# Early buffers in the room of a later weight, half score rounds and urgent adds: one change to a two-layer memory-attention kernel

## The chip, the cores and the metric

The kernel runs on one core of a Trainium2 chip. The metric is device time in microseconds (us) of one execution. A time is a median of several executions; all those quoted of the kernel before and after were in the fast state, and of the experiments all but one. TensorE, VectorE, ScalarE, GpSimd and SyncE are called PE, DVE, ACT, POOL and SP in the profile; PEld is TensorE's weight load. The granted clock is the share of TensorE's full clock that the profile's clock records show.

## The reference

x has 2048 tokens of 640 values. A layer of attention with a compressed memory (A) and a feed-forward layer with relu (B) each add to x; the pair is applied twice with the same weights.

```python
for s in range(4):                                   # segments of L = 512 tokens, 32 heads of 20
    logits = einsum('bhqd,bhkd->bhqk', qs, ks) * scale + mask
    p      = softmax(logits);  a_dot = einsum('bhqk,bhkd->bhqd', p, vs)
    pq     = phi(qs)                                 # t + 1 for t > 0, else exp(t)
    a_mem  = einsum(pq, M) / (einsum(pq, z) + 1e-06)
    o      = g * a_mem + (1 - g) * a_dot
    M, z   = M + einsum(phi(ks), vs), z + sum(phi(ks))
...
x = x + A(layernorm(x)); x = x + B(layernorm(x))     # B: relu(x @ w1) @ w2, 640 -> 1728 -> 640
x = x + A(layernorm(x)); x = x + B(layernorm(x))     # the same weights again
```

What matters here: each segment needs q, k and v, its scores and exps, a memory read (from segment 1 on) and an output projection, before the feed-forward of that segment can start. At the start of the first layer no feed-forward is ready, so TensorE has little to fill waits with.

## The kernel before

The kernel is written as some thirty streams of operations. A scheduler on the host gives each operation a modelled duration, picks at each step the one that can start first (then the one of better rank, then the stream with the lower number), and so fixes the order of every engine's instructions before the launch. An order made with modelled times is therefore part of the kernel.

```python
SEM_NS = 60.0                                # modelled time of a semaphore
...
key = (round(start), prio, n)                # smallest key goes next
```

Storage is handed out in slots; an operation that needs one waits until the last user releases it. The slots of this story:

```python
STG = [[Slot(stg[:, c, n], "stg") for c in range(FC)] for n in range(2)]   # k (n=0), q (n=1), 5 pieces each
VA = [Slot(v_aug[:, k], "va") for k in range(2)]                           # v of two segments
X = Slot(ps[:, 0:2, :], "SX")                # two PSUM banks of scores for two heads
Y = Slot(ps[:, 2:4, :], "SY")                # and two for the other two
MISC = [Slot(ps[:, 5 + k, :], "misc%d" % k) for k in range(3)]
...
sg = yield Acq([STG[n][c]])                  # proj_part: k or q of any segment
...
va = yield Acq([VA[s % 2]])                  # proj_v
```

k's staging piece is released by phi of k; that of q only when both halves of the memory read of that segment are done (`STG[1][c].release(*READ[a, s])`); v when the last heads have used it. A score round is four matmuls with 20 rows (or eight, where two key blocks share the banks), for four heads at once, followed by two exps, one for each pair of banks:

```python
def scores(m):
    ...
        yield Acq([X])
        yield Acq([Y])
        t0, t1 = yield pe(413.0, mms((0, 1, 2, 3)), pd + X.tks + Y.tks)
        for k, (bkp, tk) in enumerate(((X, t0), (Y, t1))):
            ...
            tx = yield act(1024, lambda e, dst=dst, src=src: e.activation(dst, src, ACT.Exp, scale=SCALE), [tk] + pw)
            bkp.release(tx)
```

The weights w1 and w2 of the feed-forward are loaded during the first layer, one piece after each score round's exps. A residual add (`add_half`) takes 320 columns of a PSUM bank into x on VectorE and frees the bank; an evacuation (`evac`) may go to ScalarE or VectorE, whichever is modelled to end first.

The softmax here doesn't subtract the row's maximum and nothing guards it: scores larger than these inputs give would overflow.

Of the kernel before, what the change touches and what calls it, by code (L numbers as in the profile page):

```python
# [11 lines left out]
H = 32  # L12
DH = 20
NSEG = 4
# [95 lines left out]
class Op:  # L110
# [4 lines left out]
    def __init__(self, alts, waits, dma=None, acq=None):  # L115
        self.alts = alts
        self.acq = acq
        self.waits = [t for t in waits if t is not None]
        self.dma = dma

# [18 lines left out]

class Need:  # L140
# [3 lines left out]

SEM_NS = 60.0
# [5 lines left out]
class Sched:  # L151
# [30 lines left out]
    def _settle(self, st):  # L182

        while True:
            self._fill(st)
            if st[4]:
                return False
            y = st[2]
            if isinstance(y, Op):
                return True  # L190
            if isinstance(y, Need):
                if y.key not in self.events:
                    return False
                st[2], st[3] = None, (self.events[y.key],)
            else:
                s = self._pick(y.slots)
                if s is None:
                    return False
                s.free = False
                st[2], st[3] = None, (s,)  # L200
# [20 lines left out]
    def run(self):  # L221
        while True:
            best = None
            moved = True
            while moved:
                moved = False
                for st in self.streams:
                    had = st[2]
                    self._settle(st)
                    if st[2] is not had and not isinstance(st[2], Op):  # L230
                        moved = moved or st[2] is None
            heads = [(st[0], n, st, self._alts(st[2])) for n, st in enumerate(self.streams)
                     if not st[4] and isinstance(st[2], Op)]
            for prio, n, st, alts in heads:
                ok = []
                for end, start, k, e in alts:
                    if not any(p2 < min(prio, HOLDERS) and any(e2 == e and s2 + HOLD_TOL[e] < end for _, s2, _, e2 in al2[:1])
                               for p2, _, _, al2 in heads):
                        ok.append((end, start, k))
                if not ok:  # L240
                    continue
                end, start, k = min(ok)
                key = (round(start), prio, n)
                if best is None or key < best[0]:
                    best = (key, st, end, start, k)
# [6 lines left out]
            _, st, end, start, k = best  # L252
            op = st[2]
            e, hold, fns, tail = op.alts[k]
            waits, slot = op.waits, None
            if op.acq is not None:
                slot = self._pick(op.acq)
                slot.free = False
                waits = waits + slot.tks
                fns = [(lambda eng, fn=fn, slot=slot: fn(eng, slot), mark) for fn, mark in fns]  # L260
# [20 lines left out]
def pe(ns, fns, waits=(), acq=None):  # L281
    return Op([("pe", ns, fns, 190.0)], waits, acq=acq)
# [6 lines left out]
def dve(n, mode, fn, waits=(), extra=0.0, acq=None):  # L289
    return Op([("dve", 66.0 + n / (0.96 * mode) + extra, [(fn, True)], 95.0)], waits, acq=acq)  # L290
# [6 lines left out]
def evac(n, mode, vfn, afn, waits=(), psum=True):  # L297
    return Op([("act", (52.0 if psum else 94.0) + n / 1.2, [(afn, True)], 125.0),
               ("dve", 66.0 + n / (0.96 * mode), [(vfn, True)], 95.0)], waits)
# [12 lines left out]
def bass_interleave_layers__memory_aug_infini_attn__dense_activation_relu__prompt_kernel(  # L312
    nc, A_x, A_wq, A_wk, A_wv, A_wo, A_beta, B_x, B_w1, B_w2, out,
):
    with contextlib.ExitStack() as es:
# [53 lines left out]
        STG = [[Slot(stg[:, c, n], "stg") for c in range(FC)] for n in range(2)]  # L369
# [8 lines left out]
        VA = [Slot(v_aug[:, k], "va") for k in range(2)]  # L378
# [42 lines left out]
        def late_loads():  # L421
# [16 lines left out]
            pieces += [half(k, h) for k in range(FC) for h in range(2)]  # L438
            pieces += [rows("w2", w2_r, B_w2, k) for k in range(NFULL)]
# [7 lines left out]
            for n, (name, nbytes, fn) in enumerate(pieces):  # L447
                if name not in sems:
                    sems[name] = sem_("d_" + name)
                w = yield Need("ex", *divmod(n, 5))  # L450
                tk = yield dma("sp", sems[name], nbytes, fn, w[:1] + z1, issue=400.0, lat=4500.0)
                left[name] -= 1
                if left[name] == 0:
                    S.set(name, tks=[tk])

        def consts():
# [29 lines left out]
            for b in range(2):  # L486
                VA[b].tks = [t2]
# [195 lines left out]
        def proj_part(a, s, c, n, h):  # L683
# [9 lines left out]
            if (a, s, c, n) not in QK:  # L693
                sg = yield Acq([STG[n][c]])
                QK[a, s, c, n] = (sg, [])
# [32 lines left out]

        def proj_v(a, s):
            xt = yield Need("xts", a, s)  # L730
            xt = xt[0]
            va = yield Acq([VA[s % 2]])
# [21 lines left out]
        def spill(a, s):  # L754
            for c in range(FC):
# [7 lines left out]
                for n in range(2):  # L763
# [4 lines left out]
                    scr[s % 2, 128 * c:128 * c + 128, :], stg[:, c].rearrange("p n t -> p (n t)")),  # L768
# [54 lines left out]
        def phi_(n):  # L823
            def f(a, s):
                if s == (NSEG - 1, 0)[n]:
                    for c in range(FC):
                        p = yield Need("packed", a, s, c)
                        STG[n][c].release(*p)
                    return
                done = []  # L830
                for c in range(FC):
# [3 lines left out]
                    q = stg[:, c, n, :]  # L835
# [9 lines left out]
                    if n == 0:  # L845
                        STG[0][c].release(tp)
                        if c in (2, 4):
                            S.set("phk", a, s, c // 3, tks=done)
                            done = []
# [4 lines left out]
        READ = {}  # L854

        def mem_read(hb):
            def f(a, s):
# [8 lines left out]
                for i in range(NJ):  # L866
                    fns = []
                    for z, (c, h0, h1) in enumerate(lst):
                        fns.append((lambda e, bk, c=c, h0=h0, h1=h1, z=z, i=i: e.matmul(  # L869
                            bk.ap[:, (h0 - 16 * hb) * 21:(h1 - 16 * hb) * 21],  # L870
                            stg[:, c, 1, i * 128:(i + 1) * 128],
# [16 lines left out]
                if len(READ[a, s]) == 2:  # L888
                    for c in range(FC):
                        STG[1][c].release(*READ[a, s])  # L890
                    BDS.release(*READ[a, s])
# [12 lines left out]
        def mem_write(a, s):  # L904
            mg = yield Need("maskg")
            if s < NSEG - 1:
# [3 lines left out]
                for p, cs in enumerate(PARTS):  # L910
# [4 lines left out]
                    for i in range(NJ):  # L915
                        fns = []
                        for c in cs:
                            fns.append((lambda e, b=None, c=c, i=i, o0=o0, st=(i == 0 and c == cs[0]), bk=bk: e.matmul(  # L918
                                (b or bk).ap[:, CH_OFF[c] - o0:CH_OFF[c + 1] - o0], phk[:, c, i, :],
                                v_aug[:, s % 2, i, CH_H0[c]:CH_H1[c], :].rearrange("p h e -> p (h e)"),  # L920
# [30 lines left out]
        def scores(m):  # L951
            a, r = divmod(2 * m, NSEG * G)
            s, g = divmod(r, G)
            pts = []
            sl = pd = None
            for u, parts in enumerate(ROUNDS):
                if u in (0, 2):
                    pt = yield Acq([PTS[u // 2]])
                    pts.append(pt)
                if u == 0:  # L960
                    pd = yield Need("pad", a, s, g)
                    sl, pd = pd[0], pd[1:]
                elif u == 2:
                    p1 = yield Need("pad", a, s, g + 1)
                    pd = pd + p1[1:]
                pw = [t for z, _, _ in parts for t in pts[z].tks]

                def mms(heads):
                    fns = []
                    for y, (z, j, o) in enumerate(parts):  # L970
                        N = L - 128 * j
                        for hh in heads:
                            fns.append((lambda e, z=z, j=j, hh=hh, N=N, o=o: e.matmul(  # L973
                                ps[:, hh, o:o + N], sl.ap[32 * hh:32 * hh + DH, z, 0, 128 * j:128 * j + 128],
                                sl.ap[32 * hh:32 * hh + DH, z, 1, 128 * j:L]),
                                y == len(parts) - 1 and hh in (1, 3)))
                    return fns

                yield Acq([X])
                yield Acq([Y])  # L980
                t0, t1 = yield pe(413.0, mms((0, 1, 2, 3)), pd + X.tks + Y.tks)
                ex = []
                for k, (bkp, tk) in enumerate(((X, t0), (Y, t1))):
                    if u == 2:
                        dst = PT[:, :, 2 * k:2 * k + 2, PT_OFF[2]:PT_OFF[2] + 256].rearrange("p z h q -> p h z q")
                        src = bkp.ap.rearrange("p h (z q) -> p h z q", z=2)
                    else:
                        c0 = PT_OFF[parts[0][1]]
                        dst = pts[parts[0][0]].ap[:, 2 * k:2 * k + 2, c0:c0 + 512]
                        src = bkp.ap  # L990
                    tx = yield act(1024, lambda e, dst=dst, src=src: e.activation(dst, src, ACT.Exp, scale=SCALE),  # L991
                                   [tk] + pw)
                    bkp.release(tx)
                    ex.append(tx)
                S.set("ex", m, u, tks=ex)
            sl.release(t0, t1)
# [15 lines left out]
        def apply(n):  # L1012
# [10 lines left out]
            for i in range(NJ):  # L1023
                for h2 in range(2):
                    fns = []
                    for hh in (2 * h2, 2 * h2 + 1):
                        for j in range(i + 1):
                            fns.append((lambda e, i=i, hh=hh, j=j: e.matmul(  # L1028
                                od[:, i, hh, :], pt.ap[:, hh, PT_OFF[j] + 128 * (i - j):PT_OFF[j] + 128 * (i - j) + 128],
                                v_aug[:, s % 2, j, 4 * g + hh, :], start=(j == 0), stop=(j == i)),  # L1030
# [13 lines left out]
            if g == G - 1:  # L1044
                dmt = yield Need("dm", a, s)
                VA[s % 2].release(tk, *dmt)

# [19 lines left out]
        def add_half(t, hf, bk, tk, waits=()):  # L1067
            ta = yield dve(320, 1, lambda e: e.tensor_tensor(  # L1068
                x_sb[:, t, 320 * hf:320 * hf + 320], x_sb[:, t, 320 * hf:320 * hf + 320], bk.ap[:, 0:320], ALU.add),
                [tk] + list(waits))  # L1070
# [81 lines left out]
        S.add(0, items(scores, NSEG * G))  # L1152
# [60 lines left out]
```

## Time and profile before

| | before |
|---|---|
| time, median of the first three runs | 608.51 us (608.08 to 611.05) |
| span of the profiled run | 607.5 us |
| TensorE busy | 585.3 us, 96% |
| TensorE idle, 40 to 90 us | 7.4 us |
| first feed-forward's first matmul | 111.2 us |
| mean granted clock | 0.989 |

Read it from the engine that is nearly always busy: TensorE. The amount of matmul work is fixed (6474 matmuls), so only its idle time and its low clock can be won back, and the largest piece of that lies between 40 and 90 us. The prediction below shows the lines. Two more of the kernel before are needed later. Both are of TensorE's timeline (start, duration, engine, line of the source, operation, output and input, size, count, and in brackets the idle time before it and who ended it), late in the run:

```profile
386.65 0.30 PE L525 MATMUL ps<-wo_r,oT 128*128 128x320 bf16 x1 [0.92 <-DVE x_sb L1068]
...
410.59 0.40 PE L973 MATMUL ps<-pad 20*128 20x256 bf16 x8 [1.24 <-ACT PT L991]
```

Here TensorE waits 0.92 us for a residual add to free its bank and 1.24 us for exps to free a score bank.

### The profile page before, as it was taken

To read this page: it belongs to the slowest core of one execution; us is meant where nothing else is said; L and a number is where in the kernel's file an instruction comes from. 1 tells how busy PE (TensorE), PEld (TensorE's weight loads), DVE (VectorE), ACT (ScalarE), POOL (GpSimd) and SP (SyncE) were. 2 spreads that over 40 slices of the span, in tenths; PEclk is the share of its full clock that TensorE was granted. 3 is DMA by queue.
4 is the path that set the end of the run, shared out by engine and by line. 5 is a ranking of instruction groups with operands and counts; after the bars stand their busy time and mean duration, and the time that the engine had idled before them with its cause. 6 is when DMAs were issued, how large, how long until landed. Compare 5 with 4: busy or idle time off the path is not lost.

```text
span 607.5 us, 15242 instructions
## 1 busy us (share of the span) xinstructions
PE 585.3 (96%) x6474; PEld 341.6 (56%) x6474; DVE 387.1 (64%) x1053; ACT 410.8 (68%) x520; POOL 185.7 (31%) x292
## 2 busy tenths in 40 slices
PE   7998789999999999999999999999999899999998
PEld 6664355445656554665555655456555564665655
DVE  5867789866877776876358963699636855450202
ACT  5698968978687778767868777586765867304040
POOL 4233433333434333435313442034421443100000
PEclk8999969999999999999999999999999999999999
DMA  8558974943240505611058120740214400401201
GB/s 250 133 134 225 213 162 92 215 99 63 45 151 25 89 1 159 118 31 35 11 138 149 21 44 1 201 105 1 44 36 146 90 27 12 98 34 20 67 1 44
DMA packets 100309, 53.65 MB, mean 88 GB/s; under 512 B 79186, under 2 KB 90130, under 8 KB 100242
## 3 DMA queue, kind: packets, MB, share of 16 engines
q1 hardware_dynamic: 100112, 52.52, 36.8%
q8 instruction: 51, 0.84, 0.6%
q10 hardware_dynamic: 130, 0.16, 0.1%
q14 instruction: 16, 0.13, 0.1%
HBM read 20.49 MB, written 12.85 MB: 55 GB/s over the span
## 4 chain that ended last, share of the span: by engine, by line
PE 76%; DVE 12%; ACT 5%; DMA 4%; POOL 1%; ACTq 1%; issue 1%
PE ps L528 48%; PE ps L525 10%; PE ps L1028 8%; PE ps L973 7%; ACT PT L991 3%; DVE stats L536 3%; DVE xn_tok L578 2%; DMA scr<-stg 2%; PE ps L869 1%; PE ps L918 1%; DVE x_sb L1068 1%; ACT stg L840 1%; DMA phk<-phs 1%; DVE o_sb L1039 1%; DVE om_sb L880 1%; POOL rstd L550 1%
## 5 line engine op out<-in xcount | busy, mean ns | idle before, releaser
L991 ACT ACTIVATE PT<-ps 128x1024 bf16<-128x1024 f32 x320 | 310.3, 1023 | 90.3 <-PE ps L973 85.7
L1004 POOL TENSOR_SCALAR_AFFINE_SELECT PT<-PT 128x512 bf16<-128x512 bf16 x256 | 163.5, 656 | 312.5 <-ACT PT L991 312.5
L528 PE MATMUL ps<-w_r,hT 128*128 128x320 bf16 x832 | 132.0, 299 | 0.0
L528 PE MATMUL ps<-xnT,w_r 128*128 128x512 bf16 x448 | 125.3, 379 | 0.0
L1068 DVE TENSOR_TENSOR x_sb<-x_sb,ps 128x320 bf16<-128x320 bf16 x128 | 60.8, 479 | 84.6 <-PE ps L528 84.0
L528 PEld LDWEIGHTS ps<-w_r,hT 128*128 128x128 bf16 x832 | 78.2, 98 | 33.5 <-issue 5.0
L1028 PEld LDWEIGHTS ps<-v_aug,PT 128*128 128x128 bf16 x2560 | 73.1, 96 | 9.4 <-POOL PT L1004 2.9
L1028 PE MATMUL ps<-v_aug,PT 128*128 128x21 bf16 x2560 | 74.5, 172 | 0.3 <-POOL PT L1004 0.3
L1119 ACT ACTIVATE hT<-ps 128x512 bf16<-128x512 f32 x57 | 34.1, 598 | 55.1 <-PE ps L528 54.8
L973 PE MATMUL ps<-pad 20*128 20x512 bf16 (+3 forms) x1024 | 64.0, 303 | 7.2 <-ACT PT L991 7.1
L528 PEld LDWEIGHTS ps<-xnT,w_r 128*128 128x128 bf16 x448 | 42.3, 98 | 46.8 <-issue 5.9
L536 DVE BATCH_NORM_STATS2 stats<-x_sb 128x6 f32<-128x320 bf16 x124 | 54.5, 473 | 4.6 <-DMA x_sb<-in_A_x_dram 4.2
L973 PEld LDWEIGHTS ps<-pad 20*128 20x128 bf16 x1024 | 17.8, 92 | 58.9 <-ACT PT L991 28.5
L1117 DVE TENSOR_SCALAR hT<-ps 128x512 bf16<-128x512 f32 x55 | 37.5, 684 | 18.4 <-PE ps L528 17.9
L528 PE MATMUL ps<-wo_r,oT 128*128 128x320 bf16 x256 | 47.0, 299 | 0.0
L1036 DVE RECIPROCAL rden<-ps 128x16 f32<-128x16 f32 x64 | 16.2, 253 | 43.3 <-PE ps L1028 43.1
L525 PE MATMUL ps<-xnT,w_r 128*128 128x512 bf16 x112 | 42.6, 380 | 0.2 <-DVE hT L1117 0.2
L840 ACT ACTIVATE stg<-stg 128x512 bf16<-128x512 bf16 x60 | 36.3, 638 | 9.0 <-DVE rtmp L838 8.9
L701 DVE CAST stg<-ps 128x512 bf16<-128x512 f32 (+1 forms) x46 | 28.7, 627 | 17.6 <-PE ps L528 17.4
L528 PE MATMUL ps<-wv_r,xnT 128*128 128x320 bf16 x192 | 36.2, 299 | 0.0
L528 PE MATMUL ps<-xnT,wk_r 128*128 128x512 bf16 (+1 forms) x140 | 35.0, 353 | 0.0
L528 PE MATMUL ps<-xnT,wq_r 128*128 128x512 bf16 (+1 forms) x140 | 34.6, 353 | 0.0
(85 smaller groups left out, 610.1 us busy)
## 6 DMA issues: line engine op xcount, KB each, us to landing
scr<-stg SPq DMA_DIRECT2D x39, 256.0 KB, 3.1
pad<-scr SPq DMA_DIRECT2D x124, 80.0 KB
out_dram<-x_sb SPq DMA_DIRECT2D x16, 160.0 KB, 1.8
w_r<-in_B_w_dram SPq DMA_DIRECT2D x10, 216.0 KB, 3.2
w_r<-in_B_w_dram SPq DMA_DIRECT2D x13, 160.0 KB, 3.3
x_sb<-in_A_x_dram SPq DMA_DIRECT2D x4, 320.0 KB, 5.5
x_sb<-in_A_x_dram SPq DMA_DIRECT2D x8, 160.0 KB, 3.0
wv_r<-in_A_wv_dram SPq DMA_DIRECT2D x1, 800.0 KB, 8.2
```

The costliest lines, as they stand in the source:

```text
L525: bk, tk = yield pe(mm_ns(n), [(lambda e, bk, a=a, b=b: e.matmul(bk.ap[:, 0:n] if len(b.shape) == 2 else bk.ap[:, 0:n].rearrange("p (i n) ...
L528: tk = yield pe(mm_ns(n), [(lambda e, k=k, a=a, b=b, bk=bk: e.matmul(bk.ap[:, 0:n] if len(b.shape) == 2 else bk.ap[:, 0:n].rearrange("p (i ...
L536: tk = yield dve(320, 1, lambda e, c2=c2: e.bn_stats(stats6[:, t, c2, :], x_sb[:, t, c2 * 320:(c2 + 1) * 320]), xt)
L701: te = yield evac(N, 1, lambda e, sg=sg, bk=bk: e.tensor_copy(sg.ap[:, t0:t0 + N], bk.ap[:, 0:N]), lambda e, sg=sg, bk=bk: e.activation(sg ...
L840: te = yield act(512, lambda e, q=q: e.activation(q, q, ACT.Exp), [tr] + p, psum=False)
L973: fns.append((lambda e, z=z, j=j, hh=hh, N=N, o=o: e.matmul(ps[:, hh, o:o + N], sl.ap[32 * hh:32 * hh + DH, z, 0, 128 * j:128 * j + 128], ...
L991: tx = yield act(1024, lambda e, dst=dst, src=src: e.activation(dst, src, ACT.Exp, scale=SCALE), [tk] + pw)
L1004: tm = yield pool(600.0, lambda e, reg=reg: e.affine_select(out=reg, in_=reg, pattern=[[0, 4], [1, 128]], compare_op=ALU.is_ge, fill=0.0, ...
L1028: fns.append((lambda e, i=i, hh=hh, j=j: e.matmul(od[:, i, hh, :], pt.ap[:, hh, PT_OFF[j] + 128 * (i - j):PT_OFF[j] + 128 * (i - j) + 128] ...
L1068: ta = yield dve(320, 1, lambda e: e.tensor_tensor(x_sb[:, t, 320 * hf:320 * hf + 320], x_sb[:, t, 320 * hf:320 * hf + 320], bk.ap[:, 0:32 ...
L1117: th = yield evac(512, 1, lambda e, dc=dc, bk=bk: e.tensor_scalar(hT[:, dc, :], bk.ap[:, :], 0.0, None, ALU.max), lambda e, dc=dc, bk=bk: ...
L1119: lambda e, dc=dc, bk=bk: e.activation(hT[:, dc, :], bk.ap[:, :], ACT.Relu), [tk] + HT.tks)
```

## The change

The intent is to fill TensorE's early hole. w2 is not needed until the first feed-forward has done its first half, so its space is lent: v of segment 0, and k and q of segment 1, go there. v and q of segment 2 then need not wait for the room. w2 is loaded when those have been used. Besides, a score round may go in halves: as long as the first feed-forward is not ready and TensorE would idle, and at any time when the banks of the other half are taken. And residual adds and evacuations go ahead of other work of the same modelled start. Parts of the diff, cuts marked:

```diff
+LONE_NS = 300.0
...
-                key = (round(start), prio, n)
+                key = (round(start + late), 0.5 if op.urgent else prio, n)
...
+        early_w = w2_r[:].rearrange("p c d -> p (c d)")
+        STGS = [stg, early_w[:, VLEN:VLEN + 2 * FC * L].rearrange("p (c n t) -> p c n t", c=FC, n=2)]
...
+        VAUG = [v_aug[:, k] for k in range(2)]
+        VAUG += [early_w[:, 0:VLEN].rearrange("p (j h e) -> p j h e", j=NJ, e=DH + 1)]
...
+                if n == n2:                            # the first piece of w2
+                    v0 = yield Need("v00")
+                    q1 = yield Need("q01")
+                    w2w = v0 + q1 + early_done
...
+        def vx(a, s):
+            return 2 if (a, s) == (0, 0) else s % 2
+        def sx(a, s):
+            return 1 if (a, s) == (0, 1) else 0
...
-                sg = yield Acq([STG[n][c]])
+                sg = yield Acq([STG[sx(a, s)][n][c]])
...
+                    lone = pe(413.0, [f for fs in a[2] for f in fs], a[1] + a[0].tks, take=[a[0]])
...
+                    both = pe(413.0, fns, a[1] + b[1] + a[0].tks + b[0].tks, take=[a[0], b[0]])
+                    return both, (lone if ("hx", 0, 0) not in S.events and max(ready[0], S.free["pe"]) + LONE_NS < max(ready[1], S.free["pe"]) else None)
...
-                [tk] + list(waits))                    # add_half; evac alike
+                [tk] + list(waits), urgent=True)
```

One detail of the new score stream is easy to miss: it takes "the next half and the one after it" as a pair. After an odd number of lone halves, each pair is the second half of one round and the first half of the next.

## The prediction

> **What bounds the kernel now.** I read the page first, then the busy time by stretch, then the timeline of TensorE inside the bad stretch, and the chain of waits there.
>
> ```profile
> span 607.5 us, 15242 instructions
> PE 585.3 (96%) x6474; PEld 341.6 (56%) x6474; DVE 387.1 (64%) x1053; ACT 410.8 (68%) x520; POOL 185.7 (31%) x292
> ...
> PE   7998789999999999999999999999999899999998
> ```
>
> TensorE is the bound: 96% busy, no other engine above 68%, and slices under 9 only near the start and one late. Since the amount of matmul work does not change, the kernel can only get shorter by what TensorE idles, stalls or runs at a low clock. The stretches say where that is (columns: stretch, its length, busy us of PE, PEld, DVE, ACT, POOL with counts, granted clock, DMA share, GB/s):
>
> ```profile
> 0.00:40.00 40.00, 36.46 (x383) 27.14 (x384) 26.46 (x78) 25.77 (x43) 14.49 (x31) 0.96 0.66 176
> 40.00:90.00 50.00, 42.58 (x549) 22.97 (x547) 39.40 (x114) 42.90 (x56) 20.05 (x30) 0.90 0.80 193
> 90.00:320.00 230.00, 225.63 (x2737) 126.97 (x2736) 163.88 (x435) 179.33 (x217) 83.78 (x129) 1.00 0.38 86
> 320.00:530.00 210.00, 205.88 (x2345) 119.00 (x2344) 138.97 (x384) 146.09 (x178) 66.42 (x101) 1.00 0.31 68
> 530.00:607.50 77.50, 74.75 (x468) 45.54 (x466) 18.43 (x45) 16.72 (x28) 1.01 (x1) 1.00 0.14 38
> ...
> 70.00:80.00 10.00, 6.98 (x130) 4.43 (x122) 8.37 (x29) 8.50 (x10) 4.59 (x8) 0.76 0.75 208
> 80.00:90.00 10.00, 9.81 (x109) 5.77 (x106) 7.21 (x23) 6.15 (x7) 4.00 (x6) 0.73 0.74 148
> ```
>
> Idle TensorE: 3.5 us before 40, 7.4 in 40 to 90, 4.4 in 90 to 320, 4.1 in 320 to 530, 2.8 after. In 70 to 90 the clock was also granted at 0.76 and 0.73, so (0.24 + 0.27) x 10 = 5.1 us of clock are missing. The early hole is thus worth 7.4 + 5.1 = 12.5 us, 2.1% of 608.5, if all of it comes back. The timeline shows what TensorE has to do there:
>
> ```profile
> 58.40 0.39 PE L973 MATMUL ps<-pad 20*128 20x512 bf16 x4 [1.27 <-ACT PT L991]
> ...
> 69.83 0.40 PE L973 MATMUL ps<-pad 20*128 20x256 bf16 x8 [1.09 <-ACT PT L991]
> ...
> 76.33 0.50 PE L869 MATMUL ps<-BD,stg 128*128 128x147 bf16 x3 [1.25 <-DVE om_sb L880]
> ...
> 81.33 0.45 PE L525 MATMUL ps<-wv_r,hT 128*128 128x320 bf16 x1
> ...
> 100.39 0.39 PE L525 MATMUL ps<-hT,wq_r 128*128 128x512 bf16 x1
> ...
> 110.07 0.39 PE L525 MATMUL ps<-xnT,wk_r 128*128 128x512 bf16 x1
> ```
>
> L973 is a score round, L869 the memory read. While TensorE waits for the exps at 58 to 77, the value projection of segment 2 (wv_r,hT) runs only from 81.3, its query projection from 100.4, the key projection of segment 3 from 110.1. Their inputs were there (x of segment 2 was normalized by 49); they had no room to write to. v of segment 2 needs the place of v of segment 0; q of segment 2 needs the staging of q of segment 1, which is held until the memory read is done (its last matmuls of segment 1 are at 96.6). So TensorE starves at 50 to 80 while 8 x 0.68 + 5 x 1.08 = 10.8 us of ready projections wait for buffers. The chain of waits in that stretch is ScalarE's:
>
> ```profile
> 59.38 1.83 ACT PT L991 x2
> 61.21 1.03 ACT stg L840 x2
> 62.24 1.83 ACT PT L991 x2
> ```
>
> Two exps of a round take 1.83 us, then two exps of phi 1.03. The 20 rounds of segment 0 run from 22.0 to 77.1, 2.75 us each; ScalarE is busy 50.4 of these 55 us.
>
> **The skill.** The Trainium skill, "Perfetto Trace Analysis", section Identifying the Most-Contended Engine: busy share of matmuls does not say how near TensorE is to its limit; section Optimization Strategy: repeated bubbles can mean that there is no SBUF or PSUM for the next tile. The trace agrees with both: 0.86 us for four 512-column matmuls in warm streams against 1.07 for four 320-column ones at 81.8, all called busy, and the bubbles are those of staging. "TensorE: Matmul & The Clock Gate", Part 1: idle TensorE falls back to half clock. The trace agrees: full clock until about 70, 0.76 and 0.73 right after idle gaps of 1.1 to 1.3 us in a row. The same page, Part 3: small matmuls on different row groups run at once. It agrees: a round of four 20-row matmuls holds TensorE from 58.40 to 58.73, 0.33 us for all four, and each is 388 ns long. So half a round should take as long as a whole one. The same page's table at the top: VectorE's queue is strict FIFO; no line of the trace shows VectorE's starts overtaking, so an add issued behind statistics waits for them.
>
> **The change part by part.** No matmul, exp or evacuation is added or taken away; one small GpSimd memset is new (under 1 us, GpSimd 31% busy).
>
> 1. Room. v of segment 0 and k, q of segment 1 go to w2's space. Segment 1's staging no longer waits for segment 0's, v and q of segment 2 can run from about 52. That moves 10.8 us of matmuls into 50 to 80, more than the idle there (about 7). But moving work from 81 to 110 into 50 to 80 gains nothing alone, if it leaves a hole at 81 to 110. The right question is what is left when the first feed-forward can start (110.9 now, its first matmul), because from then on there is plenty to fill with. Before: undone at 110.9 and doable earlier is only k of segment 3: 5 x 1.08 = 5.4 us (q of 3 waits for the memory read of 2, v of 3 for segment 1's heads). Its phi, spill and staging come in time for about 3.5 of 5 groups: 3.8 us.
> 2. The first feed-forward comes earlier. The output projection of segment 0 takes 86.8 to 98.1 for 8 x 0.68 = 5.4 us of matmuls, mixed with v of segment 2 (5.4 us); slack 5.8 us, I take half, 3. The exps lose 55 - 50.4 = 4.6 us of ScalarE time; of that I give halves 2. Together 5 us earlier. In these 5 us 1.8 fewer score rounds are done, about 0.8 us of TensorE each with their apply (0.33 + 0.10 switching + 1.0/2.5): -1.5.
> 3. Halves. A lone half costs TensorE another 0.33 us, but only where it idles over 0.3 us by the scheduler's plan: no cost in the hole. Once the first feed-forward is ready they are offered only when the other half's room is taken; I count 0.
> 4. Adds and evacuations first on VectorE. An add takes 0.48 us and holds one of three PSUM banks; the waits that this can shorten are the 0.5 to 1 us ones at 151, 200, 380 before wo and mem matmuls: I take 1.5 of the 8.5 us of idle in 90 to 530.
> 5. w2 last. Its 14 loads go out from 90.0 to 127.9 and its first matmul is at 158. They will now wait for the last memory read of segment 1 (96.6): about 7 us later, with the feed-forward 9 earlier the margin shrinks from 27 to some 11 us. No cost.
>
> Sum: 3.8 + 5 - 1.5 + 0 + 1.5 + 0 = 8.8 us. 608.5 - 8.8 = 599.7; I say 599.5.
>
> **The rivals.** (a) ScalarE and VectorE become the bound of the early part: in 40 to 80 they are busy 36.8 and 32.2 of 40 us, and the work moved in brings 5 x 0.60 + 8 x 0.47 = 6.8 us of evacuations, with phi of segment 2 (0.52 + 0.28 + 0.41 a piece, ten pieces, 12 us) wanting to come too. 11 us are free in both. Then exps or evacuations slip, the feed-forward comes no earlier and only part of k of segment 3 is gained: 603 to 606. For it: ScalarE at 10.0 of 10 in 60 to 70. Against: exps go first, and 30 to 40 has room too. (b) All of the hole comes back, with the clock: 12.5 us and the 1.5 of the adds, 594.5. For it: 10.8 us of ready filler against 7.4 of idle. Against: filler used there is missing at 81 to 110, where TensorE is full now only thanks to it; the idle may just move there. (c) The new order upsets the later stages (a static order made from modelled times): small waits of a us here and there, and half rounds where TensorE does have work: 606 to 610. For it: the late waits at 410 and 480 are of that kind. (d) w2 late: a wait of some us before the first second matmul of the feed-forward. Against: the 11 us of margin.
>
> **Range and chances.** 599.5 is the sum. Low end 594 is (b), high end 605 is (a). 2% is 596.3, to be had only with nearly the whole hole: 0.24. Slower by 2% would take a new stall of over 12 us, for which nothing speaks: 0.01. Within 2%: 0.75.
>
> **What would show it.** TensorE's idle in 40 to 90 under 4 us and the clock there back near 1.0 (part 1); wv_r,hT and hT,wq_r matmuls between 50 and 80; the first xnT,w_r matmul near 106, not 111 (part 2), with k of segment 3 before it; more score groups, of two matmuls each, before that time and few after (part 3); idle of 90 to 530 about 7 instead of 8.5 (part 4); no DMA wait on w2 (part 5). Wrong if a hole as large opens at 80 to 110, if the first feed-forward is not earlier, or if the stretches after 320 are longer than now.

## The result, and the profile after

| | before | after |
|---|---|---|
| median time | 609.67 us (4 runs, 608.08 to 611.05) | 603.33 us (4 runs, 601.17 to 604.4) |
| ratio of fast runs | | 0.9892, 95% interval 0.9851 to 0.9934 |
| span of the profiled run | 607.5 us | 601.9 us |
| first feed-forward's first matmul | 111.2 us | 112.5 us |
| second feed-forward's first matmul | 193.0 us | 185.6 us |

Ratios and their 95% intervals, here and below, are those of the record, from fast runs alone; they are not quite the ratios of the medians. 0.9892 is about 6.6 us: (1 - 0.9892) x 609.67. The profiled runs differ by 5.6 us.

The head of the page after:

```profile
span 601.9 us, 15245 instructions
...
PE 582.9 (97%) x6474; PEld 345.0 (57%) x6474; DVE 381.0 (63%) x1045; ACT 415.9 (69%) x528; POOL 183.9 (31%) x293
...
PE   6999979999999999999999999999999999999998
...
PEclk8999989999999999999999999999999999999999
```

The number of matmuls is as before. After the first slice only one is under 9 near the start (the 7), where there were three in a row (8, 7, 8), and the late 8 has gone. The busy time by stretch after (stretch, its length, busy us of PE, PEld, DVE, ACT, POOL with counts, granted clock, DMA share, GB/s):

```profile
0.00:40.00 40.00, 34.98 (x346) 25.61 (x346) 26.77 (x78) 25.07 (x43) 14.14 (x31) 0.96 0.67 182
40.00:90.00 50.00, 46.61 (x603) 25.24 (x604) 44.45 (x121) 44.50 (x56) 20.84 (x31) 0.96 0.83 196
90.00:320.00 230.00, 224.06 (x2755) 128.57 (x2752) 160.97 (x441) 185.00 (x223) 85.18 (x133) 0.99 0.38 89
320.00:530.00 210.00, 208.04 (x2359) 124.12 (x2357) 131.42 (x366) 144.60 (x180) 62.70 (x98) 1.00 0.30 64
...
70.00:80.00 10.00, 10.00 (x109) 4.86 (x106) 9.96 (x29) 7.73 (x10) 3.31 (x6) 1.00 0.67 186
80.00:90.00 10.00, 6.88 (x111) 3.74 (x111) 8.61 (x27) 9.29 (x12) 5.45 (x8) 0.82 1.06 226
90.00:100.00 10.00, 9.20 (x116) 5.56 (x113) 9.18 (x30) 9.01 (x13) 2.60 (x4) 0.84 0.92 214
```

TensorE idles 3.4 us in 40 to 90 instead of 7.4, and 70 to 80, the emptiest ten before (6.98 busy, clock 0.76), is full at full clock. But the next ten took its place: 6.88 busy in 80 to 90, with a clock of 0.82 there and 0.84 in the ten that follow. TensorE's timeline says what was moved and what then was missing:

```profile
53.79 0.30 PE L559 MATMUL ps<-wv_r,hT 128*128 128x320 bf16 x1
...
65.57 0.38 PE L559 MATMUL ps<-hT,wq_r 128*128 128x512 bf16 x1
...
84.39 0.39 PE L1020 MATMUL ps<-pad 20*128 20x256 bf16 x4 [1.11 <-ACT PT L1072]
...
86.59 0.50 PE L913 MATMUL ps<-BD,w_r 128*128 128x147 bf16 x3 [0.89 <-DVE om_sb L924]
87.02 0.61 PE L1020 MATMUL ps<-pad 20*128 20x512 bf16 x2
...
91.18 0.45 PE L559 MATMUL ps<-wo_r,oT 128*128 128x320 bf16 x1
...
99.43 0.31 PE L559 MATMUL ps<-wo_r,oT 128*128 128x320 bf16 x1 [0.64 <-DVE x_sb L1150]
...
100.12 0.38 PE L559 MATMUL ps<-xnT,wk_r 128*128 128x512 bf16 x1
...
112.52 0.38 PE L559 MATMUL ps<-xnT,w_r 128*128 128x512 bf16 x1 [0.70 <-issue]
...
136.62 0.30 PE L559 MATMUL ps<-w_r,hT 128*128 128x320 bf16 x1
```

The projections v and q of segment 2 (wv_r,hT and hT,wq_r) moved from 81 and 100 to 54 and 66, as intended. The key projection of segment 3 (xnT,wk_r) comes at 100.1, not 110.1, and its five groups are done before the first feed-forward (xnT,w_r); in the kernel before they ran from 110.1 to 126.7, between the feed-forward's. In 84 to 99 TensorE waits for exps, for the memory read's VectorE work and for a residual add. The groups of 4 and 2 small matmuls are lone halves. The first feed-forward is not earlier: 112.52.

w2's loads, in SyncE's list (the program's output name w_r stands for several weights):

```profile
112.00 3.68 SPq L456 DMA_DIRECT2D w_r<-in_B_w_dram  x8
...
126.39 0.56 SPq L468 DMA_DIRECT2D w_r<-in_B_w_dram  x1
```

They are issued from 112.0 to 126.4, and the first matmul that reads w2 is the last line of the timeline above, 136.6; it waited for nothing.

Why the first feed-forward is not earlier is seen where ScalarE works off the exps of segment 0. First the stretch of its 20 score rounds, before (to 77.1) and after (to 79.8):

```profile
22.00:77.10 55.10, 48.48 (x621) 27.18 (x619) 42.10 (x114) 50.46 (x67) 20.72 (x31) 0.98 0.78 189
```

```profile
22.20:79.80 57.60, 57.28 (x678) 33.24 (x678) 48.68 (x128) 49.24 (x64) 20.30 (x31) 1.00 0.77 187
```

Then the longest of what ScalarE waited for, up to and in this stretch (engine, its line, who released it: total us, times, longest), before and after:

```profile
ACT PT L991 <- PE ps L528: 3.9, 1, 3.9
ACT PT L991 <- PE ps L973: 2.2, 3, 0.8
```

```profile
ACT PT L1072 <- PE ps L1020: 7.4, 10, 2.0
```

TensorE is now full there, 57.28 of 57.6 us. ScalarE's idle time in the rounds rose from 55.10 - 50.46 = 4.6 us to 57.60 - 49.24 = 8.4, and most of the rise is exps that wait for score matmuls. The longest wait of each list, 3.9 and 2.0, lies before the first exp; within the rounds these waits rose from 2.2 us to about 5.5. The score matmuls stand in the kernel's order behind the filler. The exps of segment 0 end 2.7 us later than before. What bounded this stage was ScalarE before; in the changed kernel it is TensorE that holds it up.

That filler alone does this is not shown. The experiments below have two kernels that are as full in these rounds (TensorE idle 1.1 us in run 4, 0.9 in run 10) and in which ScalarE idles only 5.2 and 4.2 us; in run 7, which has no filler, it idles 9.3. So how full TensorE is does not decide it alone; where the score matmuls stand in the order may be the rest, which was not tested.

The rest of the way to the first feed-forward adds up so: the first output projection matmul comes 11.4 us after the last exps instead of 9.7, the projection takes 10.8 us instead of 11.3, and from its end to the feed-forward are 10.5 instead of 13.1. In the first of these stretches TensorE waits for VectorE and ScalarE, and ScalarE is busy 10.69 of the 11.4 us, where it was busy 5.08 of 9.7.

Further on, part of the early lead is given back. TensorE's stretches before and after:

```profile
210.00:350.00 140.00, 139.85 (x1704) 80.86 (x1702) 97.76 (x262) 107.60 (x130) 50.42 (x78) 1.00 0.34 72
350.00:530.00 180.00, 176.03 (x1947) 100.08 (x1945) 112.42 (x301) 122.03 (x150) 54.31 (x83) 1.00 0.29 66
```

```profile
210.00:350.00 140.00, 137.31 (x1727) 80.93 (x1724) 97.26 (x265) 109.56 (x130) 51.93 (x81) 1.00 0.32 72
350.00:530.00 180.00, 178.04 (x1928) 103.84 (x1926) 104.64 (x284) 123.30 (x158) 50.91 (x79) 1.00 0.32 68
```

Idle in 210 to 350 rose from 0.15 to 2.69 us; idle in 350 to 530 fell from 3.97 to 1.96. The new gaps stand before matmuls that need a transposed block (a DMA here):

```profile
242.92 0.98 PE L964 MATMUL ps<-v_aug,phk 128*128 128x147 bf16 x12 [1.28 <-DMA phk<-phs]
...
285.11 0.39 PE L559 MATMUL ps<-xnT,wk_r 128*128 128x512 bf16 x1 [0.72 <-DMA xnT<-xn_tok]
```

A count of the matmul work done up to each moment in the two traces puts the changed kernel 4.9 us ahead at 122 us, 6.5 at 206, 2.7 at 324 and 5.6 at the end.

### The profile page after: what moved, and what is told of

It is laid out like the page before. It is cut to its first block, busy times and chain, and to the rows that moved or that the text cites. A ratio compares the mean times of both kernels' runs of the same rounds, so it can differ in the third digit from the quotient of the medians.

```text
span 601.9 us, 15245 instructions
## 1 busy us (share of the span) xinstructions
PE 582.9 (97%) x6474; PEld 345.0 (57%) x6474; DVE 381.0 (63%) x1045; ACT 415.9 (69%) x528; POOL 183.9 (31%) x293
## 4 chain that ended last, share of the span: by engine, by line
PE 80%; DVE 10%; DMA 6%; ACT 2%; issue 1%; POOL 0%; SPq 0%
PE ps L562 50%; PE ps L559 10%; PE ps L1108 9%; PE ps L1020 7%; DMA xnT<-xn_tok 2%; DVE x_sb L1150 2%; DVE stats L570 2%; ACT PT L1072 2%; PE ps L913 1%; DVE xn_tok L612 1%; PE ps L964 1%; DMA scr<-stg 1%; DMA phk<-phs 1%; DMA oT<-o_sb 1%; DVE o_sb L1119 1%
## 5 line engine op out<-in xcount | busy, mean ns | idle before, releaser
L1084 POOL TENSOR_SCALAR_AFFINE_SELECT PT<-PT 128x512 bf16<-128x512 bf16 x256 | 160.8, 646 | 319.4 <-ACT PT L1072 319.4
L562 PE MATMUL ps<-w_r,hT 128*128 128x320 bf16 x832 | 134.5, 299 | 0.0
L562 PE MATMUL ps<-xnT,w_r 128*128 128x512 bf16 x448 | 119.9, 379 | 0.0
L1201 ACT ACTIVATE hT<-ps 128x512 bf16<-128x512 f32 x68 | 40.5, 598 | 54.5 <-PE ps L562 53.7
L1108 PEld LDWEIGHTS ps<-v_aug,PT 128*128 128x128 bf16 x2240 | 63.8, 96 | 14.5 <-issue 9.7
L1108 PE MATMUL ps<-v_aug,PT 128*128 128x21 bf16 x2240 | 68.9, 173 | 0.4 <-POOL PT L1084 0.4
L1020 PE MATMUL ps<-pad 20*128 20x512 bf16 (+3 forms) x1024 | 65.5, 303 | 2.3 <-ACT PT L1072 2.0
L1199 DVE TENSOR_SCALAR hT<-ps 128x512 bf16<-128x512 f32 x44 | 30.2, 689 | 26.3 <-PE ps L562 25.9
L559 PE MATMUL ps<-xnT,w_r 128*128 128x512 bf16 x112 | 42.6, 380 | 0.7 <-issue 0.7
L735 DVE CAST stg<-ps 128x512 bf16<-128x512 f32 (+1 forms) x43 | 26.8, 623 | 12.0 <-PE ps L562 11.5
L881 ACT ACTIVATE stg<-stg 128x512 bf16<-128x512 bf16 x50 | 30.8, 633 | 4.9 <-DVE rtmp L879 4.9
```

The source lines that it names most:

```text
L559: bk, tk = yield pe(mm_ns(n), [(lambda e, bk, a=a, b=b: e.matmul(bk.ap[:, 0:n] if len(b.shape) == 2 else bk.ap[:, 0:n].rearrange("p (i n) ...
L562: tk = yield pe(mm_ns(n), [(lambda e, k=k, a=a, b=b, bk=bk: e.matmul(bk.ap[:, 0:n] if len(b.shape) == 2 else bk.ap[:, 0:n].rearrange("p (i ...
L735: te = yield evac(N, 1, lambda e, sg=sg, bk=bk: e.tensor_copy(sg.ap[:, t0:t0 + N], bk.ap[:, 0:N]), lambda e, sg=sg, bk=bk: e.activation(sg ...
L881: te = yield act(512, lambda e, q=q: e.activation(q, q, ACT.Exp), [tr] + p, psum=False)
L1020: fns.append([(lambda e, z=z, j=j, hh=hh, N=N, o=o, sl=sl: e.matmul(ps[:, hh, o:o + N], sl.ap[32 * hh:32 * hh + DH, z, 0, 128 * j:128 * j ...
L1084: tm = yield pool(600.0, lambda e, reg=reg: e.affine_select(out=reg, in_=reg, pattern=[[0, 4], [1, 128]], compare_op=ALU.is_ge, fill=0.0, ...
```

## The experiments

Theory A was the prediction's: the room is what counts; the time is won at the start, by k of segment 3 getting out of the way of the first feed-forward. Its rivals were that the two helpers (halves, and urgent adds and evacuations) do the work, and theory L: each edit makes another static order, whose small waits fall otherwise by chance, and that is what the time shows. Twelve kernels were run; all gave the reference's result. In the edits, lines of the changed kernel carry a minus. "The room" means both places lent, that of v and that of the staging of k and q.

**Run 1: the room alone, rounds whole, nothing urgent.**

```diff
-                    lone = pe(413.0, [f for fs in a[2] for f in fs], a[1] + a[0].tks, take=[a[0]])
+                    lone = None
-                    return both, (lone if ("hx", 0, 0) not in S.events and ... else None)
+                    return both, None
-                [tk] + list(waits), urgent=True)        # and in evac
+                [tk] + list(waits))
```

> The changed kernel with its buffers in the space of w2 and w2 last, but score rounds whole again and no add or evacuation put first on VectorE. Theory A (the gain is the room: it lets k of segment 3 run before the first feed-forward, 5 x 1.08 = 5.4 us): 0.989 to 0.993 of the kernel before, that is 4 to 6.5 us faster, k of segment 3 (xnT,wk_r matmuls) done before the first xnT,w_r matmul. Theory B (the gain is the score halves and the order on VectorE; the room only moves the hole from 50-80 to 80-90): 0.997 to 1.000.

Measured: 1.0022 of before (1.0003 to 1.0041), median 610.82 against 609.13. The room alone gains nothing; theory A in its simple form has fallen. And yet its early part is there: k of segment 3 is begun at 95.6, and the second feed-forward starts at 186.1 instead of 193.0. The count of matmul work has this kernel 5.3 us ahead at 207 and 0.3 behind at 376. So the gain is made and then given back. Where is in the stretch 210 to 350, whose idle rose to 2.88 us from 0.15, and in the three longest waits of TensorE in it:

```profile
210.00:350.00 140.00, 137.12 (x1729) 78.68 (x1727) 102.68 (x270) 109.32 (x128) 52.91 (x83) 1.00 0.34 72
```

```profile
PE ps L559 <- DMA xnT<-xn_tok: 0.9, 1, 0.9
PE ps L913 <- DVE om_sb L924: 0.9, 2, 0.5
PE ps L964 <- DMA phk<-phs: 0.6, 1, 0.6
```

These are the start of the second layer: normalized x, transposed k and the memory read come to TensorE just too late for an order that runs earlier. At 368.7 there is another of the kind:

```profile
368.74 0.39 PE L559 MATMUL ps<-xnT,wk_r 128*128 128x512 bf16 x1 [1.03 <-DMA xnT<-xn_tok]
```

The added idle of 210 to 350 is 2.7 of the 5.6 us that were lost between 207 and 376, the gap at 368.7 another 1.0; where the rest went was not found.

**Run 2: both helpers, no room.**

```diff
-                if n == n2: ...
-                    w2w = v0 + q1 + early_done
+                w2w = []
...
-            return 2 if (a, s) == (0, 0) else s % 2
+            return s % 2
...
-            return 1 if (a, s) == (0, 1) else 0
+            return 0
```

> The changed kernel with the buffers and the load order of before, but halves and the order on VectorE kept. Theory A (room): 0.997 to 1.001 of the kernel before, the hole at 50 to 80 as before. Theory B (halves and order): 0.989 to 0.993.

Measured: 0.9963 (0.9945 to 0.9981), 606.88. The helpers alone gain 2.3 us. The second feed-forward starts at 195.6, so the gain is not the early one; idle in 350 to 530 fell from 3.97 to 1.70 us, the waits shown at 386 and 410 among it.

**Run 3: the change without halves.** The first two edits of run 1.

> The changed kernel with whole score rounds only. In the changed kernel only three groups of two score matmuls stand alone, but from the first one on the pairs run across rounds (six matmuls). Theory A: halves are worth nothing, the time is that of the changed kernel within 1 us (0.989 +- 0.002 of before). Rival C (the crossed pairs hurt: ScalarE lost 8.3 us in the rounds of segment 0 against 4.6 before): 2 us faster than the changed kernel, 0.985 to 0.987. Rival D (halves help as intended): 2 to 3 us slower, 0.993 to 0.995.

Measured: 0.9923 (0.9894 to 0.9952), 604.52. That is 1.9 us above the whole change (0.9923 - 0.9892 of 609), but the intervals overlap.

**Run 4: the change with nothing urgent.** The last edit of run 1.

> The changed kernel with adds and evacuations in their old rank on VectorE, halves and room kept. The prediction gave the adds 1.5 us: by it 1.5 us slower than the changed kernel, 0.991 to 0.993 of before. Rival: the new rank holds up the statistics and the first feed-forward (at 112.5 in the changed kernel, 110.9 before): 1 to 2 us faster, 0.985 to 0.988, with the first xnT,w_r matmul before 110.

Measured: 0.9892 (0.9868 to 0.9916), 603.12: the same as the whole change. On top of halves the urgent order is worth nothing that shows. But together the two are worth a lot on top of the room: 1.0022 with neither, 0.9892 with both or with halves alone, 0.9923 with urgent alone. The parts do not add up. Room alone is +0.2%, helpers alone -0.4%, both -1.1%. Any one helper keeps most of the early gain.

**Run 5: the change with phi of segment 2 held until the first feed-forward is ready.**

```diff
             def f(a, s):
+                if (a, s) == (0, 2):
+                    yield Need("hx", 0, 0)
```

> The changed kernel, with phi of segment 2 held back until the first feed-forward is ready. Its staging then stays taken, so k of segment 3 can't run before the first feed-forward; the hole at 50 to 80 stays filled as in the changed kernel. Theory A (what is gained early is k of segment 3, 5.4 us): the early lead falls from 5 us to about 0, time 0.996 to 1.000 of before. Rival F (filling the hole at 50 to 80 is itself the gain): stays at 0.988 to 0.991. Rival a of the prediction (phi and evacuations on VectorE and ScalarE hold up the first feed-forward): its first xnT,w_r matmul comes at 109 or earlier instead of 112.5.

This asks two things: whether phi's work on ScalarE and VectorE delays the first feed-forward, and what k of segment 3 ahead of it is worth, because k of segment 3 needs the staging that phi of segment 2 frees. Measured: 0.9954 (0.9938 to 0.997), 606.76. TensorE's timeline:

```profile
109.11 0.61 PE L559 MATMUL ps<-xnT,wk_r 128*128 128x512 bf16 x1
...
111.21 0.63 PE L559 MATMUL ps<-xnT,w_r 128*128 128x512 bf16 x1
```

The first feed-forward comes at 111.2 instead of 112.5. k of segment 3 is not out of the way (it starts at 109.1 and runs on to 124), the second feed-forward starts at 192.4, about as in the kernel before, and 3.8 us of the gain are gone: (0.9954 - 0.9892) x 609.84.

But the edit changed a second thing, and that leaves both questions open. The matmuls above last 0.61 and 0.63 us, those of the same shape in the changed kernel 0.38. The stretch of 90 to 130 in the changed kernel and in this run (the granted clock is the third number from the end):

```profile
90.00:130.00 40.00, 38.09 (x470) 20.65 (x466) 32.23 (x96) 35.10 (x45) 14.72 (x23) 0.96 0.63 149
```

```profile
90.00:130.00 40.00, 36.63 (x420) 18.86 (x418) 31.62 (x94) 33.32 (x42) 15.08 (x24) 0.85 0.63 146
```

The clock records have half clock from 101.9 to 112.1 us here. The mean clock of this run's 22 executions is 0.982 (none above 0.986), that of the changed kernel's four 0.990 (none below 0.989), that of the kernel before in the rounds of run 5 0.991. So the low clock belongs to this order and is no chance, and 0.8% of the time is 4.8 us, if TensorE is busy throughout: as much as was lost. How much of the 3.8 us is k of segment 3 in the way and how much the clock, this run can't tell; nor does the first feed-forward's 1.3 us bound what phi delays, since it too came after the half clock.

**Run 6: the staging's room alone; v stays in its two places.** Both helpers stay.

```diff
-            return 2 if (a, s) == (0, 0) else s % 2
+            return s % 2
...
-                    w2w = v0 + q1 + early_done
+                    w2w = q1 + early_done
```

> The changed kernel with room only for k, q of segment 1; v of segment 0 and 2 share their place as before. Theory A: q of segment 2 and so k of segment 3 are early all the same, v of segment 2 stays late but before the first feed-forward: 0.989 to 0.993. Rival F (the hole must be filled with both): half of it, 0.993 to 0.996.

Measured: 0.9848 (0.9824 to 0.9872), 600.74, 0.44% below the change itself, with intervals that overlap. The early gain is whole (second feed-forward at 184.3), and in 210 to 350 little is given back:

```profile
210.00:350.00 140.00, 139.56 (x1700) 80.03 (x1698) 95.62 (x258) 110.46 (x134) 51.02 (x79) 1.00 0.34 72
```

Idle there is 0.44 us, against 2.69 in the changed kernel.

**Runs 7, 8 and 10: the same parts in another order.** If the time is luck of the order, another order of the same parts must show another time. The planner's semaphore constant was changed, in the kernel before (run 7; with the constant left at 60 this source gives exactly the order of the kernel before), in the room alone (run 8), and in the staging's room with helpers (run 10).

```diff
-SEM_NS = 60.0
+SEM_NS = 50.0
```

> The kernel before with one constant of the host's planner changed (the assumed semaphore delay 50 instead of 60 ns), which changes nothing but the order in which ready instructions are put on the engines. Theory L (a good part of the differences is luck of the order, and the kernel before was chosen at a lucky one): 1.003 to 1.008. Theory N (order is worth nothing without new room): 0.999 to 1.001.

> The room alone, as in the run with room only, with the same constant of the planner at 50 instead of 60. Theory L with a room worth about 5 us on average: 0.990 to 0.996, against 1.002 with 60. If the room alone is worth nothing: 1.000 to 1.008 again.

> The kernel with staging room only (0.985), with the planner's assumed semaphore delay at 50 instead of 60. If 0.985 was luck of the order: 0.989 to 0.994. If giving v no room of its own is really better: 0.983 to 0.987. Early lead at 130 us of 5 to 7 us in both.

Measured: 1.001 (0.9997 to 1.0023) for before, 610.32; 1.0033 (1.0019 to 1.0047) for the room alone, 612.18, where the first order had 1.0022; 0.9845 (0.9823 to 0.9866) for the staging's room, 601.1, where the first order had 0.9848. Three pairs of orders agree within about 0.1%. Theory L does not hold at this size: luck of this kind is about 0.1% in these three pairs, and the differences between the three designs, 1.5 to 1.9%, are larger. The changed kernel itself was not run in a second order.

**Run 9: v's room alone; the staging stays.** Both helpers stay.

```diff
-            return 1 if (a, s) == (0, 1) else 0
+            return 0
...
-                    w2w = v0 + q1 + early_done
+                    w2w = v0
```

> The changed kernel with room only for v of segment 0; k, q of segment 1 are staged where they were before. Theory A: v of segment 2 runs in the hole at 50 to 80, but q of segment 2 waits for the memory read as before, so k of segment 3 comes after the first feed-forward: no early lead at the feed-forward, 0.994 to 0.998, like the run without any room (0.996). Rival F (filling the hole is the gain): early lead of some 3 us, 0.989 to 0.992.

Measured: 0.9935 (0.9911 to 0.9959), 606.32 against 611.33. q of segment 2 still waits for staging:

```profile
108.90 0.63 PE L558 MATMUL ps<-hT,wq_r 128*128 128x512 bf16 x1
```

It starts at 108.9, k of segment 3 at 118.7, and the second feed-forward at 198.2. The early gain needs the staging. The interval overlaps that of run 2, so v's room adds nothing that this run resolves.

**Run 11: the staging's room, with neither helper.** The edits of runs 1 and 6.

> Staging room only, whole score rounds, no add or evacuation first. Both kernels with all of the room and without these helpers lost their early lead again by 350 us (1.002 and 1.003). Theory G (the helpers are what keeps the lead from 200 us on): early lead 5 us, end at 0.996 to 1.002. Theory H (the extra place for v is what spends it, by changing the order later): lead kept, 0.989 to 0.993.

Measured: 0.9958 (0.9943 to 0.9973), 608.21 against 611.33. Again the early gain is made (second feed-forward 185.1) and later lost: the fourth feed-forward starts at 356.9, against 348.8 in run 6 and 353.8 in the kernel before. Idle in 210 to 350 is 3.72 us:

```profile
210.00:350.00 140.00, 136.28 (x1724) 78.06 (x1723) 101.83 (x270) 108.72 (x127) 53.69 (x83) 1.00 0.33 72
```

The helpers are worth (0.9958 - 0.9848) x 611 = 6.7 us on top of the staging's room, and (1.0022 - 0.9892) x 609 = 7.9 on top of the whole room; on top of nothing, 2.3.

**Run 12: the staging's room with the planner's constants that it rates best.**

```diff
-LONE_NS = 300.0
-SEM_NS = 60.0
+LONE_NS = 150.0
+SEM_NS = 45.0
```

> Staging room only with halves and order kept, planner constants 45 ns (semaphore) and 150 ns (how long TensorE must be idle before a lone half), the pair at which the planner's own estimate is lowest, 8 us under that of the staging kernel. If that estimate is worth something at this scale: 0.975 to 0.981. If not: 0.983 to 0.990.

Measured: 0.9862 (0.9838 to 0.9886), median 603.48 of five runs, one of them in the slow state (611.53) and left out of the ratio. The planner put TensorE's end 7.7 us earlier than in run 6 (586.8 against 594.5); on the chip nothing came of it. Runs 6 and 10 stay the best versions found.

Milestones of all runs, from the starts of matmuls in the traces (us), beside the mean granted clock of all fast executions and the ratio:

| kernel | first feed-forward | k of segment 3, first and last | second feed-forward | fourth | idle 210-350 | idle 350-530 | mean clock | ratio |
|---|---|---|---|---|---|---|---|---|
| before | 111.2 | 110.1, 126.7 | 193.0 | 353.8 | 0.15 | 3.97 | 0.991 | 1 |
| after | 112.5 | 100.1, 109.2 | 185.6 | 352.7 | 2.69 | 1.96 | 0.990 | 0.9892 |
| 1 room, no helper | 111.6 | 95.6, 108.2 | 186.1 | 356.3 | 2.88 | 3.69 | 0.991 | 1.0022 |
| 2 helpers, no room | 113.9 | 112.8, 125.0 | 195.6 | 353.4 | 0.85 | 1.70 | 0.985 | 0.9963 |
| 3 no halves | 111.9 | 95.4, 107.1 | 185.6 | 354.0 | 2.62 | 0.95 | 0.988 | 0.9923 |
| 4 nothing urgent | 111.2 | 99.6, 110.6 | 184.8 | 348.9 | 2.19 | 3.04 | 0.994 | 0.9892 |
| 5 phi held | 111.2 | 109.1, 124.1 | 192.4 | 352.7 | 1.81 | 1.11 | 0.982 | 0.9954 |
| 6 staging's room | 111.1 | 101.0, 109.8 | 184.3 | 348.8 | 0.44 | 1.97 | 0.993 | 0.9848 |
| 7 before, order 2 | 114.7 | 114.9, 128.0 | 197.2 | 356.8 | 0.95 | 4.42 | 0.990 | 1.001 |
| 8 room, order 2 | 112.2 | 87.7, 105.3 | 187.4 | 357.6 | 3.02 | 4.14 | 0.989 | 1.0033 |
| 9 v's room | 118.0 | 118.7, 132.1 | 198.2 | 354.3 | 0.10 | 1.80 | 0.983 | 0.9935 |
| 10 staging, order 2 | 109.9 | 95.9, 105.3 | 184.4 | 348.8 | 0.86 | 2.17 | 0.991 | 0.9845 |
| 11 staging, no helper | 115.0 | 102.7, 114.6 | 185.1 | 356.9 | 3.72 | 3.74 | 0.993 | 0.9958 |
| 12 staging, tuned | 109.1 | 98.8, 107.9 | 185.0 | 347.8 | 0.21 | 3.34 | 0.996 | 0.9862 |

The second feed-forward splits the kernels cleanly: 184.3 to 187.4 in all nine that have the staging's room and let phi run, 192.4 to 198.2 in the five others. That much of the mechanism is shown. The time follows it only in part, because what comes after 200 us differs by as much.

The clock column is the second thing that the time follows. The three lowest, 0.982 to 0.985, are runs 5, 2 and 9: kernels with both helpers in which k of segment 3 comes late. Against the kernel before, 0.991, they lack up to 0.9% of the time, if TensorE is busy all the while. So the helpers' 2.3 us of run 2 were gained in spite of a lower clock, and part of what separates these three from the changed kernel may be clock. Why the clock is lower in them was not tested.

What stays open. First, why the change is 0.4% behind the staging's room alone. v's place is the edit, but another thing differs with it: in the changed kernel and in runs 2 and 4, pairs of halves cross rounds to the end (111, 111 and 118 groups of 6 score matmuls), while in runs 6, 9 and 10 from about 100 us on the pairs are whole rounds again (9 to 13 such groups, all early), which is what an even number of lone halves before gives. Both could be the cause, and no run separates them. Run 12, the staging's room with crossed pairs from 73 to 364 us, lies between at 0.9862, within the interval of either. The clock alone is not the cause: it was 0.991 in run 10 and 0.990 in the change. Second, by what wait the helpers keep the lead after 200 us. Idle in 210 to 350 is 2.9 and 3.0 us in runs 1 and 8 and 3.7 in run 11, but 2.6 in run 3 too, which is faster. Idle alone does not account for it.

## Why the prediction was right or wrong

The time, 603.33, lies in the range and above the point, 599.5. By its own steps:

- **Step 1, room: right in what it does; its size is not shown.** The hole of 50 to 80 is filled, the two projections moved to where they were said to go, and all five groups of k of segment 3 come before the first feed-forward. The step was put at 3.8 us. Holding phi (run 5) takes away 3.8 us too, but with a lower clock in it, so that the two agree proves nothing. Its warning that the hole may move held too: it moved to 80 to 90. But it is a gain only with a helper (run 1), and of that the prediction said nothing.
- **Step 2, the first feed-forward 5 us earlier, less 1.5: this is the step that failed.** It came 1.4 us later (112.52). The prediction credited 2 us of ScalarE's slack to halves and 3 to a freer output projection. ScalarE lost more instead, 8.4 us against 4.6, as its exps waited for score matmuls in a full TensorE. The output projection still took 10.8 us, 91.2 to 102.0, against 11.3, with VectorE busy 9.18 of 10 us beside it. This is rival (a) in outcome, with 603 to 606 given, but only in part in cause: in the rounds TensorE was short, and not ScalarE or VectorE; in 80 to 87, where the hole now is, TensorE waits for those two, as (a) had it.
- **Step 3, halves at 0: not refuted.** 1.9 us by run 3, with intervals that overlap. The check "few after that time" was wrong in form: few lone halves, but nearly all later groups are pairs across rounds, which the prediction missed in the diff.
- **Step 4, urgent adds at 1.5 us: mis-sized.** On top of halves 0 (run 4). The waits were misread: in 90 to 530 TensorE waits for adds 1.1 us in all, 0.92 at 386.7 and 0.15 at 151.2; at 199.9 it waits for exps. Idle in 90 to 530 was to be 7; it is 5.94 + 1.96 = 7.9, from 8.5.
- **Step 5, w2 late: no cost, as said, and a margin right by luck.** No wait on w2; the last memory read of segment 1 starts at 111.5, not 96.6, and the loads went out from 112.0, the last 10 us ahead of the first use. But it was to go out 7 us later than before and went 1.5 earlier, and the first use was to be 9 us earlier (5 by step 2) and was 21.5 earlier, 136.6 against 158.1.

Two readings of the hole were off as well. The clock was not full until about 70: the trace has 0.83 in 10 to 20. And the 5.1 us of missing clock count time in which TensorE idled anyway; it was busy for 7.7 of the 10.2 us at half clock, so at most 3.9 us were to be had. Of the three signs of being wrong that the prediction named, one came true, the first feed-forward that is not earlier; the hole at 80 to 110 is 4.2 us, smaller than the 7.4 of the old one.

The sum came near by luck, because two errors met: a term of 3.5 us (5 - 1.5) that did not come, and an effect of some microseconds that was not in the sum, the helpers' keeping of the lead after 200 us. The early lead at 122 us is 4.9 us instead of the 7.3 of steps 1 and 2. Rival (c), later stages upset by the new order, describes runs 1, 8 and 11 well; chance of the order (runs 7, 8, 10) is not what it was.

## What to carry to other kernels

Filling a hole with ready work pays by what is then out of the way when the next stage begins, so count that, and look in the trace whether the filler stands ahead of the work that feeds the engine which bounds the hole. An early gain is not the kernel's gain: follow the lead along the trace to the end, and test each part of a change alone and with the others, since here the parts were worth +0.2% and -0.4% alone and -1.1% together. To tell a design from luck of its order, run the same design in a second order. And compare the granted clock before a difference is put down to the work that was moved: in run 5 the two were of one size.

## What the Trainium skill lacked or had wrong

- "Perfetto Trace Analysis", section Optimization Strategy, says of repeated bubbles that there may be no room for the next tile. That was so here, but the page does not say that room alone can be worth nothing: with the room and no other part the time was 1.0022 and 1.0033 of before in two orders (runs 1 and 8); in run 1 a lead of 5.3 us at 207 us was gone at 376.
- "TensorE: Matmul & The Clock Gate", table in Why this matters for your kernels, gives idle gaps above some 3 us as what to avoid. In the clock records of these traces the clock fell to half with far shorter gaps: from 75.2 to 85.4 us before, where no gap was over 1.3 us and idle summed to 0.70 us in the 3.4 us before it, and from 86.4 to 93.2 after, with 2.33 us in the 3.4 before it (matmul times agree: four of 320 columns took 1.07 us at 81.8 before and 0.71 at 97.4). The page's section on a second failure mode knows micro-idles as a cause, but gives no number.
- No page has how far an order planned on modelled times can be trusted. The kernel's planner put TensorE's end at 594.8 us for run 1 and 591.0 for the change, under 1% apart; the chip had them 1.3% apart. It rated run 12 ahead of run 6 by 7.7 us; the chip showed no gain (0.9862 and 0.9848).
